# RetNet and a quick-GELU MLP on one core: seven loads change queue and the first 120 works change place

## The chip, the cores and the metric

The kernel runs on one core of a Trainium2 chip. Its time is device microseconds of one execution, and it is compared by the median of several. The core has five engines, each with its own instruction stream that is worked off in order: TensorE (PE in the profile, with PEld for its weight loads), VectorE (DVE), ScalarE (ACT), GpSimd (POOL) and SyncE (SP). SP, ACT and POOL can each issue DMA transfers on a queue of their own. An instruction that has to wait for another engine, or for a transfer to land, holds up all that stands behind it on its engine.

## The reference

Two blocks follow each other. The first is a recurrent retention, for each of 4 batches and 8 heads, over 768 steps with vectors of 64:

```python
for t in range(S):
    state = gamma[None, :, None, None] * state + np.einsum('bhd,bhe->bhde', k[:, :, t], v[:, :, t])
    y[:, :, t] = scale * np.einsum('bhd,bhde->bhe', q[:, :, t], state)
```

Its output, taken as 3072 rows of 512, goes through an MLP with 2048 inner features:

```python
h = x @ w_in
g = h * (1.0 / (1.0 + np.exp(-1.702 * h)))
return (g @ w_out).astype(np.float32)
```

q, k and v are float32; the two weights come as float64.

## The kernel before

The recurrence is done in 24 steps, numbered j, each 64 time steps of two batches at once. A step of the first six (`NEW = 6`) loads three tiles of 128 x 512 float32: q, k and v of step j (`load`, line 131, with the DMA issues at L146). q and k are issued in four DMAs of 64 KB each, v in two of 128 KB; all are gathered from runs of 64 floats, 256 bytes. `plain` (line 139) takes the issuing engine as its last argument, SP if none is given. k of step 0 is issued by ACT, k of steps 1 to 5 by POOL, all q and v by SP. A tile of q, k or v has two buffers by turns, so the load of step j waits for the work of step j - 2 (for k, of the last step with the same buffers) to have read its tile.

The work of a step is cut into pieces, here called works, and each is emitted by its name:

- `turn` (L255): TensorE transposes k and q into two banks; `turned` (L266): ScalarE copies them out. `decay` (L277): ScalarE scales k, eight instructions.
- `stepJ-F`: TensorE's matmuls of `attend`: the products of q and k of step J (L294), and of step F the new share of the state (L302), the share of the old state (L311, none in step 0) and the share of the masked products (L317). `step0` has only the first, `step-0` only the second. L294 and L302 write one PSUM tile, `pa`, of which there is one, so `step1` waits until VectorE has emptied it.
- `masked` (L323): VectorE applies the decay mask to L294's result; `updated` (L371 for step 0, L373 after): VectorE adds L302's result to the state; `aged` (L362): ScalarE decays the state ahead of that; `state` (L330) and `x` (L354 for step 0, L352 after): the step's output, an input of the MLP.

Beside this runs the preparation of the first weight. Work `wPa` or `wPb` (L186) loads one 512 KB half of weight pair P, in rows of 2 KB, from SP. The float64 values are made float32 in three works: `abs` (L212, ScalarE), `half` (L216, L217, L218, VectorE) and `rest` (L222, L223, L227, VectorE). Pair 0 is done in two halves of 512 columns, `0a` and `0b`; later pairs at once, 1024 columns. There are three buffers for the raw values, so pair 3 is loaded where pair 0 was, once `rest0a` and `rest0b` are done with it. Each pair that is ready lets TensorE do matmuls of the MLP on finished rows: `up` (L417, 16 records or 8 matmuls for one work), followed by `gate` (L398).

Small tables come first (`begin`, L899 and L902): the column decays, one row of decays, and an identity for the transposes. `rows` and two matmuls called `warm` (L915, L909) are early work of TensorE; `mask` (L954) and `causal` (L919) make the mask on VectorE and POOL; `whole` (L930) loads one more small table on POOL; `table` (L952) loads ScalarE's function table.

The order of all these works, on all engines and queues at once, is a list of names in the code, which is walked once; each engine gets its instructions in the order of this list. It covers roughly the first 230 us. Behind it the order is set by loops over blocks of rows.

DMA completions are told by eight semaphores for the transfers of SP and ACT together, and eight for those of POOL, used by turns: a transfer waits at its issue for the one eight places ahead of it in its group to have landed.

Of the kernel before, what the change touches and what calls it, by code (L numbers as in the profile page):

```python
# [28 lines left out]
def kernel(  # L29
# [29 lines left out]
    pe, act, dve, pool, sp = nc.tensor, nc.scalar, nc.vector, nc.gpsimd, nc.sync  # L59
# [42 lines left out]
    rowd = const.tile([P, HP, D], F32, name="rowd")  # L102
# [3 lines left out]
    whole = const.tile([P, HP], F32, name="whole")  # L106
# [3 lines left out]
    mask = const.tile([P, 2, HP, D], F32, name="mask")  # L110
# [17 lines left out]
    NEW = 6  # L128
    QKV = {}

    def load(j, what="qkv"):

        b, c = j // NC * 2, j % NC
        rows = slice(c * D, (c + 1) * D)
        keep = tc.keep_in_program_order if j < 2 * CB else lambda i: i

        def plain(name, src, tag, bufs, engine=sp):
            t = two.tile([P, H, D], F32, name=name + "_in", tag=tag, bufs=bufs)  # L140
            QKV[name, j] = t
            for i in range(2):
                if j < NEW:
                    to, at = t[i * D:(i + 1) * D], src[b + i, :, rows, :].rearrange("h p d -> p h d")
                    for n in range(1 if name == "v" else 2):
                        keep(engine.dma_start(*((to, at) if name == "v" else (to[:, n:H:2], at[:, n * HP:(n + 1) * HP]))))  # L146
                else:
                    for r in range(2):
                        keep(engine.dma_start(t[r * D:(r + 1) * D, i * HP:(i + 1) * HP],
                                              src[b + i, r * HP:(r + 1) * HP, rows, :].rearrange("h p d -> p h d")))  # L150

        if j < NEW:
            if "q" in what:
                plain("q", q, "q_sq", 2)
            if "k" in what:
                plain("kn", k, "k_sq" if j in (0, 1, 4, 5) else "o", 2, pool if j else act)
        elif "q" in what:
            for name, src in (("q", q), ("k", k)):
                t = two.tile([P, H, D // C4, C4], F32, name=name + "_sq")
                for r0 in range(0, P, C4):  # L160
                    for n in range(D // C4):
                        t0 = c * D + n * C4
                        tc.keep_in_program_order((pool if (name, j) == ("k", 2 * CB - 1) else sp).dma_start(
                            t[r0:r0 + C4, :, n], src[b + r0 // D, :, t0:t0 + C4, r0 % D:r0 % D + C4]
                            .rearrange("h p d -> p h d")))
                QKV[name, j] = t
        if "v" in what:
            if j >= NEW and c < NC - 1:
                plain("kn", k, "kn", 1)
            plain("v", v, "v", 2)  # L170


    w1v = moe_w_in.bitcast(U32).rearrange("(c p) (f two) -> p c f two", p=P, two=2)
# [72 lines left out]
    def turn(j):  # L246

        QT[j], KT[j] = home(j, "qT"), home(j, "kT")
        if j < NEW:

            x = QKV.pop(("q", j)), QKV["kn", j]
            TURNED[j] = p = [ps.tile([P, HP, P], F32, name="pt", tag="y") for i in range(2)]
            for n in (1, 0) if j else (0, 1):
                for s in range(HP):
                    pe.matmul(p[n][:, s, :], x[n][:, 2 * s:2 * s + 2].rearrange("p r d -> p (r d)"), ident, is_transpose=True)  # L255
        else:
            for t, name in ((QT[j], "q"), (KT[j], "k")):
                tc.keep_in_program_order(dve.transpose(
                    t.rearrange("p h t -> p (h t)"), QKV.pop((name, j)).rearrange("p h n d -> p (h n d)")))
        if 2 * CB <= j < NCH - 2:  # L260
            load(j + 2, "qk")
# [113 lines left out]
    def step(j, f=None):  # L375
        attend(j, f)
        if j is not None:
            masked(j)
            if j > 2 * CB:
                decay(j)  # L380
        if f is not None:
            c = f % NC
            if c == 0:
                updated(f)
            else:
                by_state(f)
            output(f)
            if 0 < c < NC - 1:
                aged(f)
                updated(f)  # L390
        if j is not None and 2 * CB < j < NCH - 1:
            load(j + 1, "v")
# [541 lines left out]
    def late_loads():  # L934
        load(2 * CB, "qkv")
        load(2 * CB + 1, "qk")
# [58 lines left out]

    begin()
    for name in """
        k0 table q0 warm turn0 w0b rows warm k1 abs0b q1 turned0 step0 v0 w0a half0b mask k2 turn1 causal rest0b
        masked0 decay0 v1 decay1 abs0a half0a step-0 updated0 turned1 q2 step1 rowd whole w2b turn2 w2a x0 k3
        aged1 masked1 turned2 v2 rest0a abs2 q3 step-1 updated1 state1 decay2 aged2 step2 q4 x1 half2 decay3 w3b  # L1000
        w3a up0.0.0 masked2 turn3 k4 step-2 v3 q5 rest2 k5 gate0.0.0 turned3 updated2 state2 step3 up0.0.2
        masked3 abs3 half3 x2 rest3 turn4 w1b step-3 aged3 gate0.0.2 turned4 state3 w1a w5b updated3 v5 decay4
        abs1 x3 turn5 half1 up0.0.3 turned5 up0.1.2 step4 aged4 w5a rest1 v4 gate0.0.3 decay5 w6a masked4
        gate0.1.2 abs5 w6b step5-4 half5 rest5 up0.0.1 updated4 abs6 state4 gate0.0.1 w4b
        up0.1.1 half6 aged5 w4a up0.0.5 rest6 masked5 up0.1.5 gate0.1.1 x4 gate0.0.5 abs4 step-5 w8b w8a
        half4 gate0.1.5 state5 updated5 anew q6 up0.1.6 x5 rest4 gate0.1.6 abs8 v6 decay6 aged6 up0.0.6 w7b w7a half8
        turn6 gate0.0.6 up0.1.0 abs7 seven_4.2 seven_6.2 half7 gate0.1.0 w9b w9a up0.1.4 q7 gate0.1.4 step6 masked6 rest7 up0.0.4 v7
        gate0.0.4 seven_52.2 turn7 up0.1.3 gate0.1.3 step7-6 seven_4.0 masked7 updated6 decay7 aged7 abs9 state6 x6 up0.0.7 rest8 seven_w.0 gate0.0.7
        w11a w11b step-7 state7 x7 seven_x half9 w10b w10a up0.1.7 gate0.1.7
        seven2.0 seven2.1 abs11 rest9 seven2.2 seven_v.0 w12a w12b seven2.3 half11 seven2.4 abs10 seven_4.1  # L1010
        seven_w.1 seven0.0 seven2.5 rest11 seven2.6 w14b w14a seven0.1 half10 seven0.2 abs12 seven0.3 rest10
        w13a w13b seven0.4 seven_v.1 seven_4.3 half12 seven1.0 seven0.5 seven_w.3 rest12 seven0.6 abs14 seven1.1
        w15a w15b half14 seven1.2 abs13 seven1.3 seven1.4 rest14 seven_v.3 seven3.0 seven1.5 updated7 half13
        seven1.6 seven3.1 abs15 rest13 seven3.2 seven3.3 seven3.4 half15 seven3.5 late_loads rest15 seven3.6
    """.split():
        works[name]()
    ordered[0] = False
# [93 lines left out]
```

## Time and profile before

| | |
|---|---|
| median of 3 runs | 657.14 us (656.97, 657.14, 660.35) |
| the profiled execution's own time | 657.92 us |
| its span, first to last instruction | 656.2 us |
| mean granted TensorE clock | 0.995 |
| TensorE busy | 638.8 us, 97% |
| VectorE, ScalarE, GpSimd busy | 437.0, 166.4, 188.4 us |
| DMA, mean over the span | 137 GB/s |

A line of TensorE's timeline gives the start in us from the span's begin, the duration, the engine, the line of the kernel, the operation with the tiles it writes and reads, the shapes and the count of merged instructions; in brackets stands how long the engine was idle ahead of it and what it waited for. The slices of the span show tenths of busy time in 40 equal parts of 16.4 us; the row PEclk shows the clock that TensorE was granted. A DMA row gives the tile and its source, the issuing queue, the count, the size of one and the time from issue to landing.

### The profile page before, as it was taken

How to read it: one execution, taken by the hardware profiler on the slowest of the kernel's cores; microseconds unless marked ns; L12 is line 12 of the kernel's file. 1: busy time of each engine (PE TensorE's matmuls, PEld its weight loads, DVE VectorE, ACT ScalarE, POOL GpSimd, SP SyncE). 2: the span in 40 equal slices, each digit the busy share in tenths (PEclk: the TensorE clock that was granted, in tenths of full speed). 3: DMA queues.
4: the chain of work that ended last, by engine and by line, in shares of the span. 5: the costliest groups of instructions: out<-in, count | busy, mean ns of one | idle time of the engine just before them, and what ended most of it. 6: DMA issues, size and time to landing. Idle time of an engine off the chain costs nothing.

```text
span 656.2 us, 15176 instructions
## 1 busy us (share of the span) xinstructions
PE 638.8 (97%) x6390; PEld 577.5 (88%) x6390; DVE 437.0 (67%) x609; ACT 166.4 (25%) x320; POOL 188.4 (29%) x218
## 2 busy tenths in 40 slices
PE   7689999999999999999999999999999999999997
PEld 3678888888888888889999888999888999888997
DVE  3789989999936963348885246987145986144854
ACT  4664234551000000333100323110333110332210
POOL 6400341310478218000627200535300334300000
PEclk9799999999999999999999999999999999999999
DMA  9995567853233455541577821477931254501142
GB/s 178 208 247 187 141 138 218 221 120 61 50 93 148 117 155 149 193 137 41 156 163 212 244 33 49 116 191 180 262 59 49 78 158 144 204 15 49 57 153 98
DMA packets 146229, 89.77 MB, mean 137 GB/s; under 512 B 129552, under 2 KB 132368, under 8 KB 145136
## 3 DMA queue, kind: packets, MB, share of 16 engines
q1 hardware_dynamic: 133680, 44.40, 29.8%
q0 software_dynamic: 9712, 38.43, 19.0%
q10 hardware_dynamic: 2768, 5.96, 2.6%
q8 instruction: 50, 0.82, 0.5%
q14 instruction: 19, 0.16, 0.1%
HBM read 71.32 MB, written 14.94 MB: 131 GB/s over the span
## 4 chain that ended last, share of the span: by engine, by line
PE 94%; DMA 2%; DVE 2%; SPq 1%; issue 0%; ACT 0%
PE pq L717 27%; PE px L590 17%; PE pd L852 15%; PE pz L590 8%; PE ph L417 8%; PE ph L488 6%; PE py L590 4%; PE pa L294 2%; DMA W<-in_moe_w_in_dram 2%; PE pa L302 2%; PE py L317 2%; PE py L311 2%; SPq L146 1%; PE pb L488 1%; PE pt L255 0%; DVE W L218 0%
## 5 line engine op out<-in xcount | busy, mean ns | idle before, releaser
L692 POOL DMA_DIRECT2D LATE<-W2D x28 | 15.5, 553 | 245.2 <-PE pq L717 123.8
L717 PE MATMUL pq<-W,G 128*128 128x128 f32 x672 | 80.2, 276 | 0.0
L717 PEld LDWEIGHTS pq<-W,G 128*128 128x128 f32 x672 | 77.6, 192 | 0.6
L590 PE MATMUL px<-X,W1A 128*128 128x256 f32 x256 | 60.5, 379 | 0.0
L590 PE MATMUL px<-X,LATE 128*128 128x256 f32 x256 | 60.5, 379 | 0.0
L717 PE MATMUL pq<-LATE 128*128 128x128 f32 x448 | 59.8, 276 | 0.0
L417 PE MATMUL ph<-X,W1A 128*128 128x256 f32 x256 | 57.4, 382 | 2.0 <-DVE X L352 1.1
L417 PEld LDWEIGHTS ph<-X,W1A 128*128 128x128 f32 x256 | 48.0, 190 | 9.0 <-DVE X L352 1.2
L717 PEld LDWEIGHTS pq<-LATE 128*128 128x128 f32 x448 | 54.5, 192 | 0.4
L590 PEld LDWEIGHTS px<-X,LATE 128*128 128x128 f32 x256 | 48.6, 190 | 6.6
L590 PEld LDWEIGHTS px<-X,W1A 128*128 128x128 f32 x256 | 48.4, 190 | 6.5
L852 PE MATMUL pd<-W,G 128*128 128x256 f32 x224 | 49.6, 381 | 0.0
L852 PEld LDWEIGHTS pd<-W,G 128*128 128x128 f32 x224 | 42.2, 190 | 5.9
L398 ACT ACTIVATE G<-G 128x512 f32<-128x512 f32 x49 | 30.8, 629 | 45.2 <-DVE G L645 19.7
L635 DVE TENSOR_TENSOR G<-pz,vv 128x512 f32<-128x512 f32 x16 | 11.1, 691 | 46.7 <-ACT vv L605 46.6
L852 PE MATMUL pd<-W,LATE 128*128 128x256 f32 x160 | 35.2, 380 | 0.0
L852 PEld LDWEIGHTS pd<-W,LATE 128*128 128x128 f32 x160 | 30.2, 190 | 4.3 <-DVE LATE L574 0.2
L739 ACT ACTIVATE o<-pq 128x512 f32<-128x512 f32 (+1 forms) x14 | 7.6, 544 | 90.7 <-PE pq L717 90.7
L590 PE MATMUL pz<-X,W1A 128*128 128x256 f32 x128 | 30.3, 379 | 0.0
L590 PE MATMUL py<-X,W1A 128*128 128x256 f32 x128 | 30.2, 379 | 0.0
L590 PE MATMUL pz<-X,LATE 128*128 128x256 f32 x128 | 30.2, 379 | 0.0
L717 PE MATMUL pq<-LATE,G 128*128 128x128 f32 x224 | 29.6, 275 | 0.0
(211 smaller groups left out, 1175.9 us busy)
## 6 DMA issues: line engine op xcount, KB each, us to landing
LATE<-W2D POOLq DMA_DIRECT2D x28, 768.0 KB, 4.9
W<-in_moe_w_in_dram SPq DMA_DIRECT2D x12, 512.0 KB, 5.9
W<-in_moe_w_out_dram SPq DMA_DIRECT2D x10, 512.0 KB, 6.1
out_dram<-o POOLq DMA_DIRECT2D x20, 256.0 KB, 4.0
q_sq<-in_q_dram SPq DMA_DIRECT2D x144, 32.0 KB, 2.2
v_in<-in_v_dram SPq DMA_DIRECT2D x72, 64.0 KB, 2.6
LATE<-W1D ACTq DMA_DIRECT2D x3, 1536.0 KB, 7.4
LATE<-W1D POOLq DMA_DIRECT2D x3, 1536.0 KB, 8.1
```

What stands on the lines that cost most here:

```text
L294: pe.matmul(pa[HALF[w], u, 0, s, :], kt[HALF[u], w, s, :], qt[HALF[u], w, s, :], start=True, stop=True)
L302: pe.matmul(pa[HALF[u], w, 1, s, :], kd[HALF[w], HP * u + s, :], vn[HALF[w], HP * u + s, :], start=True, stop=True)
L311: pe.matmul(py[HALF[o], u, 1, 2 * w + s2, :], old[HALF[u], w, 2 * s2 + o, :], qt[HALF[u], w, 2 * s2 + o, :], start=True, stop=True)
L317: pe.matmul(py[HALF[o], w, 0, 2 * u + s2 if f < NEW else 2 * s2 + u, :], vn[HALF[w], HP * u + s, :], a[HALF[w], u, s, :], start=True, stop ...
L398: pin(act.activation(g, h[:, i], AF.Gelu_apprx_sigmoid))
L417: pe.matmul(h[:, ab], w, X[:, 2 * th + c // 2, c % 2, :], start=(ab == 0 and c == 0), stop=(c == 3), skip_group_check=True)
L488: pe.matmul(acc[:, u, :], w, x, start=(start and u == 0 and c == 0), stop=(stop and c == 1), skip_group_check=True)
L590: pe.matmul(acc[:, u, :], w1(2 * d + u, sw)[:, c, :], X[:, sx, c, :], start=(start and u == 0 and c == 0), stop=(stop and c == 1), skip_gr ...
L635: dve.tensor_add(a[3], z, v)
L692: engine.dma_start(c, W2D[i])
L717: pe.matmul(p0[:, j, :], a[:, d], w[:, d], start=(new and j == 0 and d == 0), stop=(d == NP // 2 - 1), skip_group_check=True)
L852: pe.matmul(p0[:, n, :], g1(m, p, sa)[:, n * P:(n + 1) * P], W2[:, sb, p, :], start=(new and p == 0 and n == 0), stop=(last and p == NP - ...
```

## The change

Two things change. In `load`, v of steps 0 to 5 and q of step 3 are issued by POOL's queue and no longer by SP's:

```diff
-                plain("q", q, "q_sq", 2)
+                plain("q", q, "q_sq", 2, pool if j == 3 else sp)
...
-            plain("v", v, "v", 2)
+            plain("v", v, "v", 2, pool if j < NEW else sp)
```

And the first 120 names of the list stand in a new order; from `x4` on it is the same list, broken into lines differently. In the core of it:

```diff
-        k0 table q0 warm turn0 w0b rows warm k1 abs0b q1 turned0 step0 v0 w0a half0b mask k2 turn1 causal rest0b
-        masked0 decay0 v1 decay1 abs0a half0a step-0 updated0 turned1 q2 step1 rowd whole w2b turn2 w2a x0 k3
-        aged1 masked1 turned2 v2 rest0a abs2 q3 step-1 updated1 state1 decay2 aged2 step2 q4 x1 half2 decay3 w3b
-        w3a up0.0.0 masked2 turn3 k4 step-2 v3 q5 rest2 k5 gate0.0.0 turned3 updated2 state2 step3 up0.0.2
-        masked3 abs3 half3 x2 rest3 turn4 w1b step-3 aged3 gate0.0.2 turned4 state3 w1a w5b updated3 v5 decay4
-        abs1 x3 turn5 half1 up0.0.3 turned5 up0.1.2 step4 aged4 w5a rest1 v4 gate0.0.3 decay5 w6a masked4
-        gate0.1.2 abs5 w6b step5-4 half5 rest5 up0.0.1 updated4 abs6 state4 gate0.0.1 w4b
-        up0.1.1 half6 aged5 w4a up0.0.5 rest6 masked5 up0.1.5 gate0.1.1 x4 gate0.0.5 abs4 step-5 w8b w8a
+        q0 k0 v0 decay0 table warm whole w0b k1 turn0 q1 turned0 w0a rows w2b mask warm step0 abs0b causal decay1
+        half0b masked0 abs0a turn1 step-0 w2a rest0b v1 updated0 half0a turned1 x0 k2 step1 masked1 step-1 aged1 k3
+        abs2 rest0a half2 q2 turn2 rowd q3 turned2 updated1 state1 x1 aged2 step2 turn3 decay3 masked2 v2 k4 up0.0.0
+        decay2 v3 turned3 w3a w1a w3b abs3 step-2 rest2 w1b updated2 state2 x2 step3 half3 up0.0.2 gate0.0.0 q4 turn4
+        k5 aged3 abs1 masked3 turned4 v5 step-3 q5 rest3 half1 turn5 updated3 w5a state3 w5b decay5 turned5 up0.0.3 v4
+        decay4 x3 gate0.0.2 abs5 step4 aged4 masked4 w6a rest1 w6b half5 rest5 up0.1.2 step5-4 updated4 gate0.0.3 abs6
+        masked5 half6 state4 up0.0.1 w4a aged5 gate0.1.2 gate0.0.1 up0.1.1 up0.0.5 w4b rest6 up0.1.5 gate0.1.1 x4
```

On the engines this gives, among others:

- SP issues q0, w0b, q1, w0a, w2b, w2a, q2, then the four halves of pairs 3 and 1, q4, q5, pair 5. Before it issued q0, w0b, q1, v0, w0a, v1, q2, w2b, w2a, v2, q3, q4, pair 3, v3, q5 and pair 1.
- POOL issues v0, `whole`, k1, makes the causal mask, then v1, k2, k3, q3, v2, k4, v3, k5, v5, v4. Before: k1, k2, the mask, `whole`, k3, k4, k5.
- VectorE does `updated0` ahead of `half0a`, and `mask` ahead of `half0b`.
- TensorE does turn3 ahead of up0.0.0, and turn2 behind step-1; turn1 stands ahead of step-0 as before. `step4` stands between up0.0.3 and up0.1.2.
- ScalarE does `decay0` ahead of `table`, and so loads a function table twice.

## The prediction

> **What bounds the kernel now.** I read the slices of the span first, then TensorE in order of time, then what VectorE and the DMA queues did in its pauses.
>
> The summary and the slices: TensorE is at nine tenths or more from the second slice on.
>
> ```profile
> PE 638.8 (97%) x6390; PEld 577.5 (88%) x6390; DVE 437.0 (67%) x609; ACT 166.4 (25%) x320; POOL 188.4 (29%) x218
> PE   7689999999999999999999999999999999999997
> PEclk9799999999999999999999999999999999999999
> DMA  9995567853233455541577821477931254501142
> ```
>
> The span is 656.2 us, so TensorE is idle for 17.4. Its timeline puts 13.8 of that ahead of 54.2 us and the other 3.6 behind the last matmul. The change reaches only the head (it ends at `x4`; the order behind is the same). Up to 6.6 us TensorE waits for the first loads, 3.91 and 0.64 us of idling that the new order keeps. The rest, 9.2 us, can go (0.37 before step-0 at 15.9 and the six rows below), plus what the slow clock costs: TensorE's timeline shows a block of 32 `L294` records at 1.13 us at 21.13 and at 0.64 at 26.51. The idle times, from the same timeline (start, duration, what, idle before it):
>
> ```profile
> 13.56 1.12 PE L255 MATMUL pt<-UB,kn_in 128*128 128x128 f32 x4
> ...
> 21.13 1.13 PE L294 MATMUL pa<-G 64*64 64x64 f32 x32 [4.04 <-DVE state L371]
> ...
> 28.22 3.72 PE L417 MATMUL ph<-X,W1A 128*128 128x256 f32 x16 [1.08 <-DVE X L352]
> ...
> 35.23 0.69 PE L294 MATMUL pa<-G 64*64 64x64 f32 x32 [0.62 <-DVE state L373]
> ...
> 42.35 0.69 PE L311 MATMUL py<-G,state 64*64 64x64 f32 x32 [1.28 <-DVE X L352]
> ...
> 45.47 7.17 PE L417 MATMUL ph<-X,W1A 128*128 128x256 f32 x32 [0.94 <-DVE W1A L227]
> ...
> 54.18 0.69 PE L294 MATMUL pa<-G 64*64 64x64 f32 x32 [0.91 <-DVE G L323]
> ```
>
> The largest, 4.04 us: step 1 needs the bank that `updated0` (L371) empties, and L371 stands on VectorE behind `half0a`, which waits for w0a. VectorE's timeline:
>
> ```profile
> 10.53 0.43 DVE L216 TENSOR_SCALAR W1A<-W1A 128x512 f32<-128x512 f32 x1 [9.46 <-ACT W1A L212]
> ...
> 18.39 0.66 DVE L216 TENSOR_SCALAR W1A<-W1A 128x512 f32<-128x512 f32 x1 [2.59 <-ACT W1A L212]
> 19.08 0.58 DVE L217 TENSOR_SCALAR W1A<-W1A 128x512 uint32<-128x512 uint32 x1
> 19.69 0.69 DVE L218 SCALAR_TENSOR_TENSOR W<-W,W1A 128x512 uint32<-128x512 uint32 x1
> 20.30 0.68 DVE L371 COPY state<-pa 128x512 f32<-128x512 f32 x1
> ```
>
> And the DMA issues around 8.5 and 14.6 us (count, KB, us to landing), with the busiest stretch of the head (us, PE, PEld, DVE, ACT, POOL, clock, DMA share, GB/s):
>
> ```profile
> W<-in_moe_w_in_dram SPq DMA_DIRECT2D x1, 512.0 KB, 9.2
> kn_in<-in_k_dram POOLq DMA_DIRECT2D x1, 64.0 KB, 7.4
> ...
> whole<-in_col_decay_dram POOLq DMA_DIRECT2D x1, 1.0 KB, 5.5
> ...
> 40.00:48.00 8.00, 5.78 (x121) 4.89 (x119) 7.86 (x11) 6.80 (x19) 0.00 (x0) 1.00 1.13 286
> ```
>
> The 1 KB load on POOL's queue needed 5.5 us, while the two copies of the state on the same queue at 74 us, with little else going, needed 2.3. Transfers of both queues land about in order of issue, behind everything issued earlier. This carries the sum.
>
> **The change, part by part.**
>
> *SP's queue.* It loses 12 issues of v and 4 of q3, 0.62 us each (v_in, median). That alone is worth nothing: the issues were cheap, the landing is late. But w0a, w2b and w2a now follow q1 directly at 7.1, 7.8 and 8.4 us; before, w0a left at 8.5 and w2 at 16.6.
>
> *POOL's queue.* It gains the same 16 issues. k costs 640 ns with 256 runs, `whole` 546 with 64: 0.5 ns a run, so v (512 runs) 0.77. Bounds 0.64 (as k) and 1.28 (twice k); I take 0.77, the slope between rows. First comes v0 at 3.8, then `whole`, then k1: 3.80 + 2 x 0.77 + 2 x 0.55 + 3 x 0.64 puts k1's last issue at 8.4, against 5.6 before, level with w2a. Its waits: q3 for turn1 (ends 19.7 below), v2 for step-0 (21.5), v3 for step-1 (26.4), v5 for step-2 (35.9), v4 for step-3 (42.8), and what stands behind each waits too. The line needs 12 x 0.77 + 24 x 0.64 = 25 us of issuing in 45. With 6 to 8 us to landing, v2 is there by 32 (needed at 34.3), k4, v3 and k5 by 38 (needed from 40.1), v4 by 49.4 (needed at 51.7): hidden, with about 2 us of cover; gone, each costs its lateness. Behind v4 only copies follow that had 24 us to spare.
>
> *k1 lands later.* From w0b's landing (9.84, where ScalarE starts on it) to w0a's (17.67) there landed 11 x 64 + 256 + 512 = 1472 KB: 188 KB/us. Ahead of k1's last part are now q1, half of v0 and k1 (640 KB, 3.4 us) and w0a, w2b and half of w2a (1280 KB at the 286 of the last row, 4.5 us): 9.84 + 3.4 + 4.5 = 17.7. Bounds: 13.6 (none of the weights ahead; TensorE is busy until then) and 18.6 (all of w2a). So turn1, at 13.56 before, starts at 17.7: a stall of 4.1 us in the place of the 4.04.
>
> *Down to step 1.* turn1 1.97 us (13.56 to 15.53, slow clock) to 19.7; step-0, which now stands behind it, 0.95 + 0.85 to 21.5; L371 20.65 to 21.3, no longer behind `half0a`. Step 1 starts at 21.5, against 21.13.
>
> *VectorE's line sets step 2.* After L371: half0a 1.9 (18.39 to 20.30), masked1 0.6, rest0a 1.9 (22.92 to 24.79), half2 2.6 (28.09 to 30.68), updated1 0.65: from 21.35 to 29.0. TensorE is done with step-1 at 26.4 and turn2 at 27.4 to 28.3, waits, and does step 2 at 29.0, turn3, and up0.0.0 at 30.7. Before, up0.0.0 started at 28.22 with turn3 (1.2) still to do: 1.3 behind.
>
> *The stalls after that.* By the same rows up0.0.0 ends at 34.3, step-2 at 35.9, step 3 at 36.6, up0.0.2 at 40.1, turn4 at 41.1, step-3 at 42.8, turn5 at 43.8. VectorE meanwhile: x1 to 30.3, masked2 and rest2 34.0, updated2 35.6, x2 37.3, half3 39.9 (on SP, w3, w1, q4 and q5 wait until rest0a frees a buffer at 25.7; w3b lands 8 us later and abs3 is done by 36; q5, last, leaves by 31 and is there by 38), masked3 40.5, rest3 43.6. None is late for TensorE, so the pauses of 0.62, 1.28 and 0.94 go and up0.0.3 starts at 43.8 against 45.47. Step 4 follows, up0.1.2 from 48.1 (x3 just ready) to 51.7, and step5-4 starts at 51.7 against 54.18, the 0.91 gone too: 2.5 ahead. From there both orders keep TensorE busy.
>
> *What that walk leaves out.* (a) VectorE beside POOL. L216 took 0.43 with POOL still and 0.66 with POOL issuing (16.92 to 19.40). Past half0a, four such instructions now stand beside POOL's longer line (L222, two of half2, L222): 0.2 each, 0.85; bounds 0 and 2.2 (three wait out a whole issue). The Trainium skill, "SBUF — State Buffer", section "Who interferes with whom", says that VectorE in its two-port mode and GpSimd exclude each other for a whole instruction, and its "SBUF: two separate sides" that a GpSimd-issued DMA can starve for descriptors meanwhile. The trace agrees on VectorE's side (0.43 to 0.66) and shows no stretched issue on POOL's (615 to 665 ns); by the rule in full the sum would, as an estimate, be the upper bound, 1.35 us more. (b) The clock. Before, it was granted in full from 26.3 us (the stretch 24 to 32 has a mean of 0.86: 2.3 us at half); the new order has pauses of 1.4 and 1.6 between 22 and 29, so it may stay halved until 33: bounds 0 and 2.0 (half of some 4 us of work); I take 0.9, since this is a question of phase. (c) A second table load on ScalarE (1.28), since decay0 precedes `table`: k0 landed (6.3), 2.0, 1.3 and 0.2 give 9.8 for turned0, done at 10.9, and step 0 waits for the warm matmul until 12.5 anyway: nothing, with 1.6 us of cover.
>
> **Sum:** -2.5 + 0.85 + 0.9 = -0.75 us. On the profiled execution 657.92 (span 656.2, 1.7 around it) that is 657.2; that run lies 0.8 above the median, 657.14, so the median becomes **656.4**.
>
> **The rivals.**
>
> *POOL's loads pass the weights (faster).* If k1 does not queue behind w0a and w2, turn1 starts at 13.6. Next in line is the landing of v1 and k2, issued only from 13 us on, which takes about 1 us back: 3 us better than the sum, **653.4**. The Trainium skill, "DMA: Bandwidth & Descriptors", section "Queues, rings and completion order", says that each DMA engine takes turns between queues packet by packet, which is this rival. Against it: the 1 KB load on POOL's queue that took 5.5 us.
>
> *POOL's queue becomes the pace (slower).* One queue now issues 36 loads of q, k and v, v with twice k's runs. If an issue of v takes 2.5 us rather than 0.77, the line needs 12 x 2.5 + 24 x 0.64 = 45 us of issuing behind its start at 3.8, so v4, needed at 51.7, lands some 7 us after its issue at about 49: 4 to 5 us late, **661.1**. It decides from about 2 us a v on. For it: no row shows an issue of 512 runs on this queue; against it: the slope of 0.5 ns a run.
>
> *Nothing moves net*: the two stalls of 4 us exchange and the rest cancels. That is the upper part of my own case.
>
> **How the numbers follow.** 0.5% is 3.3 us, about what a measurement of this kernel can tell from no change (its three runs span 3.4). My case and its bounds reach from 653.9 (no price for a and b) to 660.0: chance 0.66, all within. Loads that pass: 0.15, faster. POOL as the pace, or stalls of that size behind it: 0.19, slower. The range 653.4 to 661.1 goes to the middle of both rivals and leaves out about 0.17.
>
> **What would show it.** turn1's first L255 on k1 starting near 17.7 with an idle of about 4 named DMA kn_in or POOL; step 1 near 21.5, and L371 directly behind L227 on VectorE; step 2 near 29; no idle of over 0.6 on TensorE past 31; L216 and L222 longer beside POOL; v's issue on POOL near 0.77. A turn1 at 14 makes the first rival right, a v issue over 2 us the second; a new TensorE pause past 31 us, or a slow clock past 33, breaks the walk.

## The result, and the profile after

| | before | after |
|---|---|---|
| median | 656.96 us (22 runs, 655.32 to 660.35) | 659.88 us (22 runs, 657.41 to 662.26) |
| the profiled execution's own time | 657.92 us | 660.03 us |
| its span | 656.2 us | 658.3 us |
| TensorE busy | 638.8 us | 640.7 us |

The ratio of after to before is 1.0037, with a 95% interval of 1.0026 to 1.0049. By the ratio the change costs 2.4 us (the two medians lie 2.9 us apart). That is less than the 0.5% which the forecast called about no change, but clearly of the other sign than the 0.75 us it promised.

The summary and three rows of the slices, from the page of the changed kernel:

```profile
PE 640.7 (97%) x6390; PEld 579.1 (88%) x6390; DVE 435.5 (66%) x609; ACT 167.9 (26%) x321; POOL 197.4 (30%) x234
...
PE   5879999999999999999999999999999999999997
...
PEclk9989999999999999999999999999999999999999
DMA  8996577863233556541466921386941253601142
```

At this scale TensorE's row differs in the first three slices alone. By its timelines all that differs lies ahead of 57 us: from there on the two kernels run alike to within 0.1 us. TensorE's timeline of the changed kernel (start and duration in us, line, tiles, count; in brackets the idle time ahead and its releaser):

```profile
17.08 1.09 PE L255 MATMUL pt<-UB,kn_in 128*128 128x128 f32 x4 [3.29 <-DMA kn_in<-in_k_dram]
...
23.19 1.13 PE L302 MATMUL pa<-v_in,G 64*64 64x64 f32 x32 [1.06 <-DVE G L323]
...
28.29 0.69 PE L294 MATMUL pa<-G 64*64 64x64 f32 x32 [0.98 <-DVE state L373]
...
29.85 3.62 PE L417 MATMUL ph<-X,W1A 128*128 128x256 f32 x16
33.40 0.33 PE L302 MATMUL pa<-v_in,G 64*64 64x64 f32 x4
34.83 0.67 PE L302 MATMUL pa<-v_in,G 64*64 64x64 f32 x26 [1.10 <-DMA v_in<-in_v_dram]
37.21 0.26 PE L302 MATMUL pa<-v_in,G 64*64 64x64 f32 x1 [1.71 <-issue]
...
40.06 3.72 PE L417 MATMUL ph<-X,W1A 128*128 128x256 f32 x16
...
48.10 0.63 PE L255 MATMUL pt<-UB,q_in 128*128 128x128 f32 x4 [1.28 <-DMA q_in<-in_q_dram]
48.57 3.62 PE L417 MATMUL ph<-X,W1A 128*128 128x256 f32 x16
...
56.40 0.69 PE L294 MATMUL pa<-G 64*64 64x64 f32 x32
```

Down to up0.0.0 (L417 at 29.85) the walk of the prediction holds to 0.9 us. Then three pauses follow that it did not have, of 1.10, 1.71 and 1.28 us. Step5-4 starts at 56.40, against 54.18 before: 2.2 us later, about the measured loss. Behind it TensorE is busy without a break in both kernels, up to the last matmul.

In sum the pauses hardly changed: past 12 us they are 9.2 us before and 9.4 after, of which the last three are 4.1. Most of the 2.1 us between the two executions is busy time, 638.8 and 640.7 us, so slower work. By the traces the clock was at half up to 16.0 and from 19.4 to 26.3 us before, and up to 26.4 and from 36.6 to 40.0 after.

The pauses stop VectorE too, and they cost the clock. VectorE's timeline at the same place, and the busy times of the stretches from 26 us on (us; PE, PEld, DVE, ACT, POOL; granted clock, DMA share, GB/s):

```profile
32.18 1.23 DVE L227 TENSOR_TENSOR W1A<-G 128x1024 f32<-128x1024 f32 x1
37.68 0.69 DVE L373 TENSOR_TENSOR state<-state,pa 128x512 f32<-128x512 f32 x1 [4.28 <-PE pa L302]
```

```profile
26.00:34.00 8.00, 6.75 (x74) 5.53 (x70) 7.27 (x9) 6.84 (x24) 4.99 (x8) 1.00 1.04 250
34.00:42.00 8.00, 5.47 (x133) 5.00 (x134) 3.30 (x5) 3.10 (x7) 3.21 (x5) 0.79 1.15 194
42.00:50.00 8.00, 6.72 (x128) 5.83 (x127) 7.83 (x10) 5.80 (x16) 2.10 (x3) 1.00 1.04 230
```

Between 34 and 42 us the clock's mean is 0.79 (it is halved from 36.6 to 40.0), and the DMA engines are full at 194 GB/s, while VectorE is busy for 3.30 of 8 us. So loads are late, and not because the engines have too little asked of them.

SP's timeline and its waits show which:

```profile
24.95 1.91 SPq L186 DMA_DIRECT2D W<-in_moe_w_in_dram  x4
27.35 15.22 SPq L146 DMA_DIRECT2D q_in<-in_q_dram  x8
```

```profile
SPq L146 <- DMA W<-in_moe_w_in_dram: 5.7, 3, 3.5
```

The four halves of weights w3a, w1a, w3b and w1b leave SP together at 24.95 to 26.9. The eight issues of q4 and q5 behind them, 5 us of work at 0.62 each, take 15.2. With eight semaphores in turn, the four issues of q5 wait for the four weights, eight places ahead: 5.7 us in three waits. One more issue, at 32.09, itself took 3.93 us; why is not shown. By the trace w3b landed at 37.87 and w1b at 41.95; the last two issues of q5 left at 37.89 and 41.97. q5 landed at 47.97, turn5 started on it at 48.10, and up0.0.3 behind it at 48.57 (before: 45.47).

### The profile page after: what moved, and what is told of

It is laid out like the page before. It is cut to its first block, busy times and chain, and to the rows that moved or that the text cites. A ratio compares the mean times of both kernels' runs of the same rounds, so it can differ in the third digit from the quotient of the medians.

```text
span 658.3 us, 15189 instructions
## 1 busy us (share of the span) xinstructions
PE 640.7 (97%) x6390; PEld 579.1 (88%) x6390; DVE 435.5 (66%) x609; ACT 167.9 (26%) x321; POOL 197.4 (30%) x234
## 4 chain that ended last, share of the span: by engine, by line
PE 93%; DMA 5%; POOL 1%; DVE 1%; issue 0%; SPq 0%; POOLq 0%
PE pq L717 27%; PE px L590 17%; PE pd L852 15%; PE pz L590 8%; PE ph L417 8%; PE ph L488 6%; PE py L590 4%; DMA W<-in_moe_w_in_dram 2%; PE pa L294 2%; PE pa L302 1%; PE py L317 1%; PE py L311 1%; DMA kn_in<-in_k_dram 1%; PE pb L488 1%; DMA q_in<-in_q_dram 1%; PE pt L255 0%
## 5 line engine op out<-in xcount | busy, mean ns | idle before, releaser
L417 PE MATMUL ph<-X,W1A 128*128 128x256 f32 x256 | 57.5, 382 | 0.0
L417 PEld LDWEIGHTS ph<-X,W1A 128*128 128x128 f32 x256 | 47.9, 190 | 6.7
```

Of the source, the lines that this page charges most:

```text
L417: pe.matmul(h[:, ab], w, X[:, 2 * th + c // 2, c % 2, :], start=(ab == 0 and c == 0), stop=(c == 3), skip_group_check=True)
```

## The experiments

Each run is compared with the kernel before on the same chip. The mark is the start of L302 in step5-4, in one profiled execution: 54.66 before, 56.91 after. Before has its first late weight on SP at 29.30 and up0.0.3 at 45.47. The clock's turn falls differently in each execution (below). Behind the mark, too, executions differ: before and after run alike there, but in e2 another 1.1 us and in e17 2.1 us go at a few places near 338, 351 and 439 us. So the mark tells of one execution, and the ratio decides. In e3, e6, e7, e10 and e12 pair 1 leaves later than the column for the weights says, in e17 w1b does.

The expectations name their theories by letters. A: the backlog of weights makes the loads behind them late. B: the queues cost something by themselves. C: the early pause ahead of turn1, with the clock, is the loss. S: the two queues share the DMA engines. O: loads land in order of issue. D: w1b's landing holds q5.

| run | edit | median us | ratio, 95% interval | weights leave SP | up0.0.3 | mark |
|---|---|---|---|---|---|---|
| after | the change | 659.88 | 1.0037 (1.0026, 1.0049) | 24.95 | 48.57 | 56.91 |
| e1 | its queues alone | 658.39 | 1.0015 (0.9998, 1.0032) | 24.63 | 44.63 | 53.82 |
| e2 | its order alone | 656.83 | 0.9993 (0.9975, 1.0011) | 25.04 | 43.77 | 52.51 |
| e14 | after, v2 to v5 on SP | 659.11 | 1.0033 (1.0018, 1.0048) | 27.44 | 46.77 | 55.51 |
| e15 | after, v0 and v1 on SP | 657.52 | 1.0004 (0.9989, 1.0018) | 22.11 | 45.32 | 53.66 |
| e3 | after, pair 1 late | 658.46 | 1.0007 (0.9988, 1.0026) | 24.17 | 45.26 | 54.91 |
| e17 | after, w1b late | 659.32 | 1.0020 (1.0000, 1.0041) | 23.34 | 48.48 | 57.04 |
| e9 | before, pair 1 early | 656.57 | 0.9991 (0.9975, 1.0006) | 29.89 | 43.66 | 52.75 |
| e4 | after, q3 on SP | 658.13 | 1.0013 (0.9995, 1.0031) | 24.10 | 46.97 | 55.87 |
| e5 | e4, and q5 on POOL | 660.51 | 1.0042 (1.0024, 1.0059) | 23.47 | 46.49 | 54.84 |
| e11 | e4, and q4 on POOL | 659.53 | 1.0030 (1.0013, 1.0046) | 24.15 | 46.77 | 55.11 |
| e6 | e3 and e4 | 657.01 | 0.9995 (0.9973, 1.0017) | 23.60 | 44.91 | 53.39 |
| e8 | after, k1 first, pair 2 later | 662.40 | 1.0071 (1.0046, 1.0097) | 21.33 | 48.06 | 56.84 |
| e7 | e6, e8, turn2 ahead of step-1 | 657.89 | 1.0013 (0.9989, 1.0038) | 23.41 | 44.26 | 53.26 |
| e10 | e6, pauses filled | 656.62 | 0.9988 (0.9975, 1.0001) | 22.52 | 44.22 | 52.99 |
| e12 | e2, pair 1 late, pauses filled | 657.19 | 0.9996 (0.9980, 1.0012) | 25.60 | 43.24 | 52.86 |
| e13 | before, updated0 first | 656.68 | 1.0000 (0.9984, 1.0016) | 28.90 | 42.34 | 51.53 |
| e16 | e13, and q3 on POOL | 657.79 | 1.0011 (0.9999, 1.0022) | 25.05 | 43.76 | 52.95 |

### The two halves of the change: e1 and e2

e1 has the new queues with the old list of works, e2 the new list with all v and q3 on SP.

> The changed queues (v of steps 0 to 5 and q3 on POOL) with the order of before. Theory A (the backlog: in the changed order four halves of weights leave SP at 24.95 to 26.4 us, together with v2, k4 and v3 on POOL, so v2, k4 and q5 land 9 to 15 us after their issue): the old order spreads the weights (w3b, w3a, then pair 1 behind turn4), so v2 is there in time and the time is that of before, 656.5 to 657.5. Theory B (v and q3 on POOL cost something by themselves: VectorE beside POOL, runs moved as other packets): the loss of 2.4 us is here too, 659 to 660. Theory C (the pause before turn1 and the phase of the clock): turn1 comes at 13 to 14 as before, so no loss, 656.5 to 657.5.

> The changed order with the queues of before (v and q3 on SP). Theory A: v2 now stands ahead of the weights on SP's own queue and cannot be passed by them, so the pauses of 1.10 and 1.71 us before step-2 go, but SP carries 16 more issues of 0.62 us; 657 to 658.5. Theory B: without POOL's extra loads the loss is gone, 656 to 657. Theory C: turn1 still waits until about 17, so the loss stays, 659.5 to 660.5.

The order alone is not slower than before, and it is 0.44% better than the whole change. Its walk ends where the predicted one does: step5-4 starts at 52.00, where 51.7 was forecast, though turn1 starts at 14.21 and not at 17.7. The mark lies 2.15 us ahead of before's. Only little of that shows in its ratio, 0.9993 with 0.0018 on either side, so no gain is shown. The queues alone cost 1.0 us, with an interval that includes zero. The two add up to 0.5 us, not to 2.4. With the intervals as they are, the 1.9 us between are just outside the noise, so most of the loss seems to need both.

TensorE's line of e2 at turn5 and up0.0.3, to set beside those of the changed kernel at 48.10 and 48.57:

```profile
42.70 0.60 PE L255 MATMUL pt<-UB,q_in 128*128 128x128 f32 x4
43.77 3.72 PE L417 MATMUL ph<-X,W1A 128*128 128x256 f32 x16 [0.47 <-DVE W1A L227]
```

### Which loads of v: e14 and e15

```diff
-            plain("v", v, "v", 2, pool if j < NEW else sp)
+            plain("v", v, "v", 2, pool if j < 2 else sp)              # e14
+            plain("v", v, "v", 2, pool if 1 < j < NEW else sp)        # e15
```

> The changed kernel with v of steps 2 to 5 back on SP; v0, v1 and q3 stay on POOL. Theory S (POOL's loads run beside SP's weights from 25 us on and take the DMA engines from them): the late traffic is now that of the order alone, but for q3; v2 leaves SP ahead of the weights; 656.5 to 658. Theory C (the early pause before turn1, which comes from v0 ahead of k1 on POOL): turn1 still starts at about 17, the loss stays, 659 to 660.

> The changed kernel with v of steps 0 and 1 back on SP; v2 to v5 and q3 stay on POOL. Theory S: the late traffic is that of the changed kernel, so v2, k4, q4 and q5 are as late and the loss stays, 658.8 to 660.5. Theory C: k1 is first on POOL, turn1 starts by 14.5, and the loss goes: 656.5 to 658.

This went against theory S, as it stood: with v2 to v5 back on SP the loss stays, with v0 and v1 back it goes. In e15 turn1 starts at 13.35 instead of 17.08 and the weights leave SP at 22.11 instead of 24.95. The issues of q on SP are still held, and turn4 waits 1.33 us for q4, but the last issue of q5 comes 1.7 us earlier and up0.0.3 3.3 us:

```profile
22.11 2.60 SPq L186 DMA_DIRECT2D W<-in_moe_w_in_dram  x4
28.37 12.45 SPq L146 DMA_DIRECT2D q_in<-in_q_dram  x8
```

```profile
44.85 0.63 PE L255 MATMUL pt<-UB,q_in 128*128 128x128 f32 x4 [0.17 <-ACT G L277]
45.32 3.62 PE L417 MATMUL ph<-X,W1A 128*128 128x256 f32 x16
```

e15's last issue of q5 left at 40.23. In e14 turn1 waits until 16.09, step-1 comes at 22.03 (20.14 in e2), and v3, which now stands ahead of the weights on SP and waits for step-1's buffer, holds them until 27.44. So the loss needs v0 and v1 on POOL. How they bring it about is not shown. That v0 stands ahead of k1 there, and makes turn1 late, can't be all: e8 below puts k1 first, turn1 starts at 13.53, and the loss is larger. Nor is it the time at which the weights leave SP: in e2 that is 25.04, and e2 loses nothing.

### The four halves of weights: e3, e17 and e9

In e3 pair 1 is issued behind q5 and not among the halves of pair 3, in e17 only w1b is; abs1 and half1 follow.

```diff
-... w3a w1a w3b abs3 step-2 rest2 w1b updated2 ... aged3 abs1 masked3 turned4 v5 step-3 q5 rest3 half1 turn5 ...
+... w3a w3b abs3 step-2 rest2 updated2 ... aged3 masked3 turned4 v5 step-3 q5 w1a w1b rest3 turn5 ... turned5 abs1 ...
```

> The changed kernel with w1a and w1b issued behind q5 (SP: w3a w3b q4 q5 w1a w1b) and abs1, half1 later. Theory A: 1 MB less stands ahead of k4, v3, q4 and q5; they land about 3.6 us earlier (1 MB at 286 KB per us), the 1.28 us before turn5 and the late abs3 go; v2 still has two halves of weights ahead of it, so the 1.10 and 1.71 us stay: 658 to 659. If both queues share the DMA engines evenly instead of landing in order of issue, v2 gains too: 657 to 658. Theory C: no change, 659.5 to 660.5.

> The changed kernel with one 512 KB transfer moved: w1b is issued behind q5, w1a stays between w3a and w3b (abs1 and half1 behind it, as with the whole pair). In the changed kernel q5's last issue left SP at 41.97, when w1b had landed at 41.95, eight transfers earlier in the count of SP's semaphores; q5 landed at 47.97 and turn5 started on it at 48.10. Theory D (that chain sets the end): q5's last issue then waits for w3b at most (37.9), lands by 43 to 44, the 1.28 us before turn5 go, up0.0.3 starts at 44.9 to 46 instead of 48.57; 657 to 658. If only the bytes of the whole pair matter, half of the gain of the run with pair 1 late: 658.5 to 659.2.

e3 takes 0.30% off the change and is not different from before. The pause ahead of turn5 is gone:

```profile
44.82 0.60 PE L255 MATMUL pt<-UB,q_in 128*128 128x128 f32 x4
45.26 3.62 PE L417 MATMUL ph<-X,W1A 128*128 128x256 f32 x16
```

v2 is late as in the changed kernel: 0.74 us, and the pause named "issue" behind it stays with 0.67. That agrees with theory A. In this execution two others came: 0.99 us, again "issue", at 42.78, and 1.25 us for ScalarE at 50.74.

e17 settled the chain that it asked about, but not the time: its 659.32 misses theory D. q5's last issue left at 35.91, no longer held by w1b, and nothing waited for q5. But in its profiled execution, at 662.33 the slowest of its ten, TensorE stood still for 4.84 us in another place. TensorE's and POOL's timelines of e17:

```profile
32.83 1.09 PE L255 MATMUL pt<-UB,q_in 128*128 128x128 f32 x4 [4.84 <-DMA q_in<-in_q_dram]
```

```profile
22.43 2.96 POOL L146 DMA_DIRECT2D q_in<-in_q_dram  x4 [0.36 <-PE pa L302]
25.38 1.36 POOL L146 DMA_DIRECT2D v_in<-in_v_dram  x2
```

Here the weights left SP at 23.34, 1.6 us sooner than in the changed kernel's execution, and so ahead of half of q3 on POOL: its parts landed at 24.70, 27.78, 30.92 and 32.74, where in the changed kernel all four were there within 2.3 to 3.0 us of their issue. By these landings 1 or 2 us decide which of the loads that TensorE needs next falls behind the weights. This run's times spread from 656.40 to 662.33.

e9 puts pair 1 into the same place in the kernel before, and changes nothing else:

```diff
-        w3a up0.0.0 masked2 turn3 k4 step-2 v3 q5 rest2 k5 gate0.0.0 turned3 updated2 state2 step3 up0.0.2
-        masked3 abs3 half3 x2 rest3 turn4 w1b step-3 aged3 gate0.0.2 turned4 state3 w1a w5b updated3 v5 decay4
+        w3a w1b w1a up0.0.0 masked2 turn3 k4 step-2 v3 q5 rest2 k5 gate0.0.0 turned3 updated2 state2 step3 up0.0.2
+        masked3 abs3 half3 x2 rest3 turn4 step-3 aged3 gate0.0.2 turned4 state3 w5b updated3 v5 decay4
```

> The kernel before with one edit: w1b and w1a are issued directly behind w3a, ahead of v3 and q5, as the changed order does it. Theory A: 1 MB more stands ahead of v3 and q5 on SP; at 200 to 286 KB per us they land 3.7 to 5 us later, v3 at 42 to 43 instead of 38.2, and step-3, which started at 40.38, waits about 2 us for it: 1 to 2.5 us slower than before. If the loss needs POOL's longer queue or the pause before turn1, the time stays that of before within 0.5 us.

A miss for theory A, and a useful one: the four halves, one behind the other, cost nothing here. v3 landed at 40.42 and held step-3 by two pauses of under 0.3 us. The views of the DMA show what differs; that this is the reason is my reading. First e9, then the changed kernel, each in a stretch in which weights move (queue, packets, MB, share of the 16 engines; q1 is that of SP, q0 that of POOL):

```profile
DMA packets 831, 1.55 MB, mean 388 GB/s; under 512 B 86, under 2 KB 86, under 8 KB 830
...
q1 hardware_dynamic: 830, 1.53, 103.0%
```

```profile
DMA packets 163, 0.35 MB, mean 220 GB/s; under 512 B 41, under 2 KB 41, under 8 KB 162
...
q0 software_dynamic: 81, 0.18, 62.1%
q1 hardware_dynamic: 81, 0.16, 39.8%
q8 instruction: 1, 0.02, 5.7%
```

With POOL's queue silent, SP's weights move at 1.53 MB in 4.0 us (33 to 37). Beside POOL's loads they move 0.16 MB in 1.6 us (34.0 to 35.6), about a quarter of that rate, and both queues together are at 220 GB/s and not at 388. That need not come from the second queue. POOL's loads are gathered from runs of 256 bytes, and where SP's queue alone moves such runs the rate is as low, here in before from 34 to 38.5 us:

```profile
DMA packets 2245, 0.82 MB, mean 182 GB/s; under 512 B 2102, under 2 KB 2102, under 8 KB 2244
...
q1 hardware_dynamic: 2244, 0.80, 100.8%
```

In before POOL had issued its last k by 26.1 and the weights left at 29.3. The change moves 16 loads to POOL and brings the weights forward to 25 us, into the middle of them.

### The weights against v2, q4 and q5: e4, e5, e11 and e6

```diff
-                plain("q", q, "q_sq", 2, pool if j == 3 else sp)
+                plain("q", q, "q_sq", 2)                                 # e4
+                plain("q", q, "q_sq", 2, pool if j == 5 else sp)         # e5, and q5 behind k5 in the list
+                plain("q", q, "q_sq", 2, pool if j == 4 else sp)         # e11, and q4 behind k4 in the list
```

> The changed kernel with q3 back on SP's queue, all else the same. POOL then issues v2 at about 22.4 instead of 24.83 us, ahead of all four halves of weights. Theory A: v2 lands by 28, the pauses of 1.10 and 1.71 us before step-2 go and with them the second stretch of slow clock (36.6 to 40.0): 656.5 to 658. Theory B: four loads fewer on POOL, a few tenths: 659 to 660. Theory C: the pause before turn1 stays, no change: 659.5 to 660.5.

> As the run with q3 on SP, and q5 issued by POOL behind k5 (at about 33 us) instead of by SP. There SP's q4 left at 27.0 and landed at 41.8 while k5 on POOL left at 32.3 and landed at 40.6. Theory S (the two queues share the DMA engines, so a load on the emptier queue passes the other queue's backlog): q5 lands at 41 to 42 instead of 45, and the pause of 1.94 us before turn5 falls under 0.7; 656.8 to 657.8. Theory O (loads land in order of issue whatever the queue, as the prediction had it): q5 stands behind the same bytes, lands at 44 to 46, the pause stays; 658 to 658.5.

> As the run with q3 on SP, and q4 issued by POOL behind k4 instead of by SP behind the four halves of weights. In that run q4 left SP at 27.0 to 29.0 and landed at 41.8 to 42.4, and turn4 waited 1.94 us for it. Theory S (the queues share): q4 leaves at about 27 to 29.5 and lands by 38.5, the pause before turn4 goes; 656.5 to 657.8. Theory O (order of issue): it lands at 40 to 42 as before, the pause stays over 1 us; 658 to 658.8.

In e4 v2 left at 22.08 and landed at 28.44, so nothing waits for v2. It is 0.24% better than the change, with intervals that overlap, and less than theory A said: two pauses remain. TensorE's lines of e4:

```profile
35.05 0.21 PE L302 MATMUL pa<-v_in,G 64*64 64x64 f32 x1 [1.45 <-issue]
...
42.98 0.63 PE L255 MATMUL pt<-UB,q_in 128*128 128x128 f32 x4 [1.94 <-DMA q_in<-in_q_dram]
```

The second of these is turn4's, for q4. I read it as turn5's when I wrote e5, so e5 moved a load that nobody was waiting for. Its q4 still landed at 42.37 and turn4 still waited, for 1.27 us. But q5 shows the passing: its first part left POOL at 32.65 and landed at 40.93, ahead of the first part of q4, which had left SP at 27.27 and landed at 41.05. e11 moved the right load: q4 landed at 35.99 to 38.15 instead of 41.8 and later, and turn4 starts without a pause. So theory S is right in this: a load on the emptier queue passed the other's backlog. Neither run is faster for it (1.0042 and 1.0030, where e4 had 1.0013). ScalarE's line of e11 shows one reason, abs1 waiting for w1b ahead of turned4:

```profile
41.32 1.20 ACT L212 ACTIVATE W1A<-W 128x1024 f32<-128x1024 f32 x1 [1.74 <-DMA W<-in_moe_w_in_dram]
42.60 1.08 ACT L266 ACTIVATE G<-pt 128x512 f32<-128x512 f32 x2
```

e6 joins e3 and e4: pair 1 late, q3 on SP.

> Both single edits at once: q3 on SP (so v2 leaves ahead of the weights) and w1a, w1b behind q5. Theory A (backlog of weights ahead of v2, q4 and q5): the pauses before step-2 and before turn5 both go, TensorE reaches step5-4 about 2 us earlier than in the kernel before (54.66 us for its L302); 655.5 to 656.8. If the loss is elsewhere: no better than the better of the two alone, 658.

Past up0.0.0 TensorE has no pause of over 0.4 us, and the loss is gone: 0.9995, 0.42% better than the change. The mark lies 1.27 us ahead of before's, the ratio shows no gain. SP's line, to be read against the 15.22 of the changed kernel:

```profile
23.60 0.89 SPq L186 DMA_DIRECT2D W<-in_moe_w_in_dram  x2
27.75 6.29 SPq L146 DMA_DIRECT2D q_in<-in_q_dram  x8
```

### The early pause and the clock: e8, e7, e10 and e12

e8 has k1 ahead of v0 on POOL and pair 2 behind q2 on SP; e7 has this, all of e6, and turn2 ahead of step-1.

```diff
-        q0 k0 v0 decay0 table warm whole w0b k1 turn0 q1 turned0 w0a rows w2b mask warm step0 ...
+        q0 k0 k1 v0 decay0 table warm whole w0b turn0 q1 turned0 w0a rows mask warm step0 ...
-        half0b masked0 abs0a turn1 step-0 w2a rest0b ...
+        half0b masked0 abs0a turn1 step-0 q2 w2b w2a rest0b ...
-        abs2 rest0a half2 q2 turn2 rowd ...
+        abs2 rest0a half2 turn2 rowd ...
```

> The changed kernel with k1 ahead of v0 on POOL and w2b, w2a behind q2 on SP only. Theory A: turn1 starts near 14, the pause of 3.29 us goes, but v2, q4 and q5 are as late as before, so most of the gain is lost by the pauses at 34 to 48 us: 658.5 to 660. Theory C (the early pause is the loss): 656 to 657.5.

> The last one, and k1 ahead of v0 on POOL, w2b and w2a behind q2 on SP, and turn2 ahead of step-1 on TensorE. Theory A with the early pause as a cost of its own: turn1 starts near 14 instead of 17, the pause of 1.06 before step-1 is filled by turn2, TensorE is at step5-4's L302 by 50 to 51 us; 653 to 655.5. If the pauses only change place (the 4 us return at step 1, because the weights land later, as between before and after): 656 to 657.

In e8 turn1 starts at 13.53, without a pause, and the run is the slowest of all, 1.0071. The pause moved to the loads that now come later: 1.91 and 1.37 us ahead of step-1 for v1, 2.05 in turn3 for q3. The full clock came at 16.0 and was lost again from 19.4 to 36.5. e7 gets back to 1.0013; there turn2 waits 5.05 us for k2. Both miss their theory.

e10 adds to e6 four unused matmuls of the kind of `warm` in TensorE's pauses, e12 three of them to e2 (with pair 1 late; the first pair of lines is e10's alone):

```diff
-... abs0a turn1 step-0 ...
+... abs0a warm turn1 step-0 ...
-... step1 masked1 step-1 ...
+... step1 masked1 warm step-1 ...
-... aged2 step2 turn3 ...
+... aged2 warm warm step2 turn3 ...
```

> The run with q3 on SP and pair 1 late, and four more of the early matmuls that write a bank nobody reads: one ahead of turn1, one ahead of step-1, two ahead of step 2, in TensorE's pauses. They compute nothing that is used. Theory C' (stretches of 3.41 us in which TensorE pauses keep or take the clock): the full clock comes by 15 to 18 us instead of 32.3 and stays; up0.0.0 and step-2 run at full speed; TensorE is at step5-4's L302 1 to 2 us sooner (53.39 there), 655 to 656.5. If TensorE's own order is not what sets the pace there (VectorE's line is), the L302 comes at the same time within 0.5 us, or up to 1 us later.

> The changed order with the queues of before, pair 1 behind q5, and the same unused matmuls ahead of step-1 (one) and step 2 (two). With the order alone the clock was at half from 20.4 to 30.7, behind a stretch in which TensorE paused 1.78 us. Theory C': the clock stays full from 17 us on, TensorE is at step5-4's L302 at 50 to 51.5 instead of 52.5; 654.5 to 656. If VectorE's line sets the pace: 52 to 53, 656 to 657.

The clock followed: in e10 it was full from 14.8 us instead of 32.3 and at half only from 25.0 to 28.4, in e12 it was full from 16.8 and at half only from 23.6 to 27.0 (in e2 from 20.4 to 30.7). The mark did not: 52.99 against 53.39, and 52.86 against 52.51. up0.0.0 starts at 31.05 in e10 and at 31.23 in e6. So a faster clock that early did not bring TensorE ahead; it waited longer, in e10 2.17 us at 24.50 in one pause named "issue". What set the pace instead was not tested. e10 has the lowest ratio of all, 0.9988, with an interval that just reaches 1.

### The largest pause of before, alone: e13 and e16

```diff
-... abs0a half0a step-0 updated0 turned1 ...
+... abs0a step-0 updated0 half0a turned1 ...
```

e16 has this and q3 on POOL's queue.

> The kernel before with one edit of its order: updated0 (L371) stands ahead of half0a on VectorE, all else as before. Step 1 then need not wait for the weights and starts at 17 to 18 instead of 21.13. If the pause of 4.04 us was on the path that sets the end: step5-4 comes 2 to 3 us sooner than 54.66, 654 to 655.5. If VectorE's line behind it sets the pace (half0a still waits for w0a until 18.4, then masked1, rest0a, half2, updated1): the pauses only move behind step 1, 656.5 to 657.8.

> The kernel before, with updated0 ahead of half0a (as in the run of that edit alone) and q3 on POOL's queue. In that run turn3 paused 2.61 us for q3, whose last issues on SP waited until 25.3 to 28.8 for weights to land. If POOL issues q3 by 23, it lands by 29, and turn3, step-2 and what follows come up to 2 us sooner than there: step5-4's L302 at 49.5 to 51, the median 654.5 to 656.2. If VectorE's line (rest3 ahead of up0.0.3) or the landing of pair 3 sets that part: no better than 51.5 and 656.5.

In e13 step 1 starts at 18.20 instead of 21.13, and up0.0.0 at 24.00 instead of 28.22: 4.2 us sooner. The time is the same, 1.0000. TensorE's lines say where it went:

```profile
30.77 0.63 PE L255 MATMUL pt<-UB,q_in 128*128 128x128 f32 x4 [2.61 <-DMA q_in<-in_q_dram]
...
34.41 0.69 PE L294 MATMUL pa<-G 64*64 64x64 f32 x32 [1.45 <-DVE state L373]
```

With q3 on POOL (e16) the first of these goes, 1.85 us appear at 30.41, and the second grows to 2.14. In the profiled execution of e13 the mark is 3.1 us ahead, and most of that lasts to the end, but that execution is the fastest of its ten (655.16, the median 656.68). Of all that was taken out of the early pauses, no median shows a gain.

## Why the prediction was wrong

**Right, by its own steps.** The issue of v on POOL took 0.70 us (0.77 was taken). k1's last issue came at 8.14 (8.4), turn1 started at 17.08 (17.7), step 1 at 20.99 (21.5), L371 stood directly behind L227 at 20.16, step 2 came at 28.29 (29.0), up0.0.0 at 29.85 (30.7). The second table load cost nothing: turned0 ended at 12.3 and the warm matmul at 12.7. The price (a) was too high: beside POOL L216 took 0.58 and 0.81, L222 0.42 and 0.90, some 0.5 us over the rows without POOL, not 0.85. "POOL's queue becomes the pace" is refuted by the 0.70.

**Wrong: the landings past 25 us.** The step that failed is "hidden with about 2 us of cover". It gave every load 6 to 8 us to landing. v2 was to be there by 32 and landed at 34.78, 9.0 us after its issue; k4, v3 and k5, promised by 38, landed as late as 45.4; "q5, last, leaves by 31 and is there by 38": it left at 41.97 and landed at 47.97. The walk counted issues, and took the landing time from a stretch in which less was under way. By the prediction's own rate it could have been seen: from 24.8 to 30.9 there leave v2, four halves of weights, k4, q4 and v3, 3.0 MB, which at 286 KB per us are 10.7 us, and at the 194 of the stretch from 34 to 42 us 16.

**Wrong: what a wait on SP holds.** The eight semaphores are told of in the description of the kernel, and the walk did not use them. The four issues of q5 wait for the four weights ahead of them to land, 5.7 of the 15.2 us that 5 us of issuing became.

**Wrong: "none is late for TensorE".** From up0.0.0 at 30.7 to step5-4 at 51.7 the walk had no pause; measured were 29.85 and 56.40. The 4.7 us between are: -0.85 at the start, 1.10 + 1.71 + 1.28 of pauses, and the second stretch of half clock, 3.4 us at about 0.8 busy, 1.4. That adds up to 4.6. Of the pauses two, 2.38 us, are loads that landed late; the 1.71 is not a load of the kernel's (last section). The term (b) of the sum had priced a slow clock until 33 with 0.9; it came back at 26.4 and was lost again at 36.6, by the new pauses.

**Half right: the rival "POOL's loads pass the weights".** At turn1 it did little: k1's last part, issued at 8.14, landed at 16.84, ahead of w2b, issued at 7.75 and landed at 17.41, but turn1 still waited 3.29 us. Past 25 us it holds, and it brought no gain: k4 left POOL from 26.55 on, behind w1b on SP at 26.39, and was there by 38.4, w1b at 41.95. I had set the 1 KB load of 5.5 us against this rival. The Trainium skill, "DMA: Bandwidth & Descriptors", section "Queues, rings and completion order", says that each DMA engine takes turns between the queues packet by packet. The landings of e5 and e11 agree with the page.

**What is shown and what is not.** Shown is that the loss needs two parts: v0 and v1 on POOL's queue (without that, e15, it is gone) and the weights of pair 1 in that place (without them, e3 and e6, it is gone). e9 has pair 1 early with the queues of before, e3 has the queues without pair 1, and neither differs from before. The queues in the old order (e1) stand at 1.0015 with an interval up to 1.0032, so a part of the loss may be theirs. That w1b's landing holds q5 is read in the trace, and e17, without it, agrees; that this made the last 1.28 us of the profiled execution is read, too. How v0 and v1 bring the loss about stays open. So does which of the late loads costs most in an average execution: e5, e11 and e17 each met another one.

## What to carry to other kernels

A load that is moved to an earlier place or another queue needs the bytes ahead of it counted, on all queues, at the rate of that stretch, and not a landing time from another one. Put large transfers that are needed late behind small ones that are needed soon, also where the queue would be free for them: here one megabyte, whose first matmul stands behind step5-4 and so some 30 us later, cost 2.0 us (the changed kernel against e3). In e9, with fewer other loads under way, the same megabyte cost nothing. A pause that is taken out early in a pipeline can come back behind it, as in e13; look first for what waits next.

## What the runs showed of the hardware

**The clock goes in stretches of 3.41 us.** Wherever a trace has more than one change of the clock, the changes lie multiples of 3.41 us apart, on a grid that lies differently in each execution. No border in TensorE's busy share comes out of these traces. The full clock came at the end of stretches that were 83 to 100% busy (in the changed kernel 93%, up to 26.4), but not after 88% in e2 (up to 23.8), nor after a stretch of 100% in before (9.2 to 12.6). It was lost after 53% and less (35% in the changed kernel, up to 36.6; 53% in e12, up to 23.6) and once after 68% (e15, up to 11.6); it stayed full after 47% in e4, 50% in e7 and 53% in e17. In e2 two pauses that make 1.78 us in one stretch were enough to lose it. The Trainium skill, "TensorE: Matmul & The Clock Gate", section "Part 1: The HAM clock gate", gives the same window, free-running, and an idle one as the condition for half; in these runs a half-idle one did it.

**TensorE seems to stop for its own instructions.** The pause of 1.71 us with the releaser "issue" in the changed kernel is not v2's: e4, where v2 had landed 5 us ahead, has it with 1.45, at the same matmul, the 341st. In the stretch from 34.0 to 35.6 shown above, a packet of the instruction queue (q8, 16 KB) was on the DMA engines. In the traces of e4, e6, e11 and e17 such a packet, which takes 0.9 to 1.5 us, ends 1.35 to 1.66 us ahead of the end of each pause of this kind. Two of these pauses, in e17, lie far behind the mark, 0.54 us at 355.4 and 0.36 at 443.4. All this is read from the timing; no run tested it.

**Runs of 256 bytes go with about half the rate, on one queue as on two.** 388 GB/s for the 2 KB rows of the weights alone (e9, 33 to 37 us); 220 for the weights beside the 256-byte runs of POOL's loads (the changed kernel, 34.0 to 35.6); 182 on SP's queue alone, where most packets were of 256 bytes (before, 34 to 38.5).
